# Keys of the first two tiles through unfolded weights, weights turned by DMA, layernorm roots in pairs, and a new port model in the scheduler, in a two-layer linear-attention and gated-MLP kernel

**Chip, cores, metric.** One core of one Trainium2 chip. The metric is the device time of one execution in microseconds (us), median of the runs; lower is better.

## The reference, cut to what matters

Inputs are bfloat16: x of 2048 x 512 (16 tiles of 128 rows), 32 heads of 16.

```python
def A(x, wqkv, w_phi, wo):                    # linear attention with learned features
    q, k, v = split(x @ wqkv)                 # heads of 16
    pk = k @ w_phi                            # per head 16 x 16; the same for q
    phi_k = concat(softmax(pk), softmax(-pk)) # 32 features a head
    kv = phi_k.T @ v ;  z = phi_k.sum(rows)   # sums over ALL 2048 rows
    return (phi_q @ kv) / (phi_q @ z + 1e-6) @ wo
def B(x, W_gate, W_up, W_down):
    return (relu(x @ W_gate) * (x @ W_up)) @ W_down
x += A(layernorm(x)); x += B(layernorm(x))
x += A(layernorm(x)); x += B(layernorm(x))
```

No query can be finished before the last of the sixteen key tiles is summed. The first key stage is therefore a wall: all attention outputs and the first gate matmul lie behind it.

## The kernel before

The kernel first records all its operations (engine, cost, priority, what they depend on, buffers). A list scheduler then sets the order on each engine with a cost model, and a table of some 2,100 priorities (DUE) found by search steers it. A string of bits (PLACE) says which of two engines takes each operation that can run on either. So a change of the model, the tables or one operation can move any instruction anywhere.

w_phi is folded into the key weights: `Wk2 = wk @ Wblk`, for which wk must be turned first. Before, TensorE turns it:

```python
k_fold = fold(wk, Wk2, l_wk, 100, 100, ("ACT", "DVE"))   # 16 turning matmuls, 4 copies ("hT<-b"),
                                                         # 16 folding matmuls, 4 copies ("Wk<-b")
def norm_A(l, t, due, after, how):            # one tile at a time
    a = stats(l, "A", t, due, after)          # VectorE: bn_stats, bn_aggr
    a = op("ACT", ACT1, due, lambda: nc.scalar.activation(out=ln[:, t:t + 1], in_=mv[:, t, 1:2], func=AF.Ln, ...
    a = op("ACT", ACT0, due, lambda: nc.scalar.activation(out=rs[:, t:t + 1], in_=ln[:, t:t + 1], func=AF.Exp, scale=-0.5)...
    n = op("DVE", SCALE, due, lambda: nc.vector.tensor_scalar(out=xn.t[:], in0=x_of(t), ...   # "xn"
    return turn(xn, ...)                      # tiles 0-3 by TensorE, the others by DMA from SyncE
class Keys:
    def tile(self, t, ...):
        k = op("PE", mm(4, 512), ...  kp = xnTA @ Wk2                    # "K"
        e = [op("ACT", act(512), ...  ek[s] = exp(+-kp)  for s in 0, 1   # "ek"
        v = op("PE", ... vp = xnTA @ wv ; evac(...)                      # "vext", ScalarE or VectorE
        a = op("DVE", SUM16, ...      sk = sum16(ek)                     # "sk", the softmax sums
        a = op("ACT", ...             sk = exp(-ln(sk))
        a = two multiplications phiK = ek * sk, each on VectorE or GpSimd
        z = op("PE", SUMS, ...        q += phiK.T @ vext                 # "kvz", the key sums
    def build(self, due):             # R: the key sums, laid out for the queries; 8 VectorE instructions
        for k in range(2):
            for s in range(2):
                made.append(op("DVE", ..., num, self.sums + [c_r1], ...)); made.append(op("DVE", DVE0, ..., den, ...))
def attend(...):                      # "erq" waits for all eight
    pe.append(op("PE", mm(len(groups), GE), due, ..., eq + made, [ps], name="erq"))
# the scheduler's port: one lock for VectorE's two-port forms and GpSimd
t = max(clock[e], o.ready, port if o.port else 0.0, ...);   port = t + occ
```

Cut: query projections, MLP, second layer, evacuations.

The softmax here doesn't subtract the row's maximum and nothing guards it: scores larger than these inputs give would overflow.

Of the kernel before, what the change touches and what calls it, by code (L numbers as in the profile page):

```python
# [8 lines left out]
P = 128  # L9
D = 512  # L10
H = 32
DH = 16
# [24 lines left out]
class Op:  # L37
# [3 lines left out]
    def __init__(self, eng, cost, due, emit, deps=(), takes=(), uses=(), name="", move=0, port=False,  # L41
                 follow=(), alt=None):
        self.eng, (self.occ, self.lat) = eng, cost
        self.due, self.emit, self.name, self.move, self.port = due, emit, name, move, port
        self.deps = [d for d in deps if d is not None]
        self.follow = [d for d in follow if d is not None]
        self.takes, self.uses = list(takes), list(uses)
        self.then, self.behind, self.alt, self.twin = [], [], alt, None
# [24 lines left out]
HOP = {"PE": 50, "ACT": 32, "DVE": 32, "POOL": 165, "SP": 90}  # L73
COLD = 3500
LANES = 8
# [3 lines left out]
def plan(ops):  # L79
# [14 lines left out]
    while len(order) < len(ops):  # L94
# [9 lines left out]
        for e, cand in open_.items():  # L104
            first, at = None, []
            for o in cand:
                t = max(clock[e], o.ready, port if o.port else 0.0, lanes[0] if o.move else 0.0)
# [11 lines left out]
            if first is None or (best is not None and first > best[0]):  # L119
                continue  # L120
            o = min((o for t, o in at if t <= first + 1), key=rank)
            came = max(clock[e], o.ready)
            if best is None or first < best[0] or came < best[1]:
                best = first, came, o
        assert best is not None, "no instruction can go"
        t, _, o = best
# [11 lines left out]
        if o.port:  # L138
            port = t + occ
# [68 lines left out]
SUMS = (8 * 40, 8 * 40 + 170)  # L208
# [4 lines left out]
XPOSE, XPOSE_LOADS = (1200, 3600), (1200, 3600)  # L213
# [3 lines left out]
def dma(nbytes):  # L217
    return 460, 2000 + nbytes / RATE


class K:
# [9 lines left out]
    "0000010100000000000000000000000001000000000001000000010000010000111000100010000011100010000000001100"  # L231
    "1110100001101000000001001111110001111111000111101111011101100100001001010011001101100101101011001010"
    "0111100111000000000111000001000000011010011000110100110100010010010010011111011011010111101111110001"
    "1"
)
PHI = dict(POOL=("POOL", "POOL"), DVE=("DVE", "DVE"), BOTH=("DVE", "POOL"))
PHI0 = ["POOL", "POOL", "DVE"] * 5 + ["BOTH"]
BLOCKS = ((1, 1, 2, 4, 4, 2, 2), (1, 1, 2, 4, 4, 2, 1, 1))
# [4 lines left out]
    171312045, 171176422, 171176382, 171108352, 171198950, 171077496, 171191852, 171044825, 171078679, 171078698,  # L243
    171075562, 172890511, 176979114, 171233483, 169157194, 169158347, 169158293, 172028606, 169159557, 172030067,
    175144900, 173911508, 175144538, 171845769, 169157815, 171893840, 172460034, 171325700, 171787868, 171042634,
    171000808, 171921057, 170984535, 171039910, 171020854, 171061543, 170544187, 171018809, 171804656, 171138113,
    171042055, 171921054, 166325450, 171843476, 171894266, 172913174, 172651099, 171841824, 172662070, 171803244,
    170856605, 171671995, 171013294, 171049523, 171011469, 170882211, 170861860, 170773832, 171088096, 171173941,
    166032751, 171021263, 171024027, 165980719, 171010636, 170972794, 170819202, 170901748, 170120315, 170882262,
    171029170, 171058781, 171028664, 170882214, 170773339, 170644736, 171176421, 170834144, 170500271, 171024600,  # L250
    171023816, 171671545, 170881567, 170973450, 170924320, 170862256, 171733328, 171027555, 171028689, 170104438,
    170987569, 171023551, 171017586, 170995073, 171010979, 171010010, 167097015, 171025767, 171021114, 170976230,
    171009963, 170940900, 170707416, 170903149, 170861679, 170895382, 170987736, 170805774, 171134539, 171029304,
    171015238, 170840189, 171086712, 170868324, 172856244, 171023850, 170972541, 170882265, 170862137, 170938874,
    171078382, 171074459, 171076295, 170781572, 171024964, 171027552, 170806858, 171027495, 171045955, 171031024,
    170994249, 171063885, 171044941, 170994211, 171021566, 171025728, 170861672, 170773342, 171004053, 171050973,
    171041308, 166032748, 171017859, 170995571, 172857251, 170995217, 171021462, 171036003, 171036000, 171021133,
    171034376, 171019328, 171026473, 170901529, 171024967, 170970509, 170994580, 171076245, 171039727, 174124623,
    167096153, 170995703, 170993965, 172856241, 171391510, 169375356, 166303781, 170203837, 171046298, 171045973,
    171020654, 171025772, 171029618, 171031289, 171018943, 171009668, 171040302, 212653769, 170870934, 170529933,  # L260
    171034876, 170993625, 171023605, 170674343, 170471544, 170946591, 173676712, 171046899, 170942347, 170973537,
    170992325, 171016031, 171004733, 170995129, 171046905, 171039117, 171046765, 170882142, 171036586, 171036549,
    170994607, 171035366, 171017772, 171035774, 166304101, 171351583, 171019187, 170346706, 170971352, 171020568,
    171004375, 171003406, 171019334, 170304741, 171357616, 166452149, 166304120, 171079347, 166362383, 171167760,
    171117024, 166253921, 166338723, 171040796, 171047078, 171026685, 169377831, 171021245, 170994356, 170993118,
    36276708, 36035224, 170174038, 170250060, 171018957, 171021288, 171052769, 171039826, 171052600, 171024073,
    170912232, 170912229, 171041278, 171041091, 171026709, 170998266, 170996907, 171023919, 171166970, 170791395,
    170174888, 36033968, 171014267, 166253845, 171052882, 170955784, 170370511, 171069861, 171052009, 171114979,
    171018524, 171021870, 166290380, 169376343, 170080981, 170529851, 171023791, 170744874, 36538735, 169932483,
    167242939, 166340952, 169222540, 171015285, 166253698, 171075807, 171049021, 171048078, 171040769, 171046830,  # L270
    170951770, 171034112, 171019616, 162145965, 166306292, 168062450, 170989765, 170738642, 171014079, 171052180,
    171053152, 171029348, 171107467, 171116988, 171052395, 171052101, 171047241, 171018507, 166291021, 170394652,
    170241606, 169841292, 169839339, 171025410, 36538707, 169011552, 170955744, 171035785, 170982203, 171011859,
    172910993, 171019677, 171107459, 171053563, 171019442, 170965939, 171116604, 170396198, 170371650, 170946958,
    170908940, 171025481, 169342071, 170739641, 170936868, 171053246, 171052141, 170955698, 171107296, 170969038,
# [183 lines left out]
def kernel(  # L459
# [14 lines left out]
    def pool(name, n, shape, dt=BF16, fifo=False):  # L474
        return Pool([new(f"{name}{i}", shape, dt) for i in range(n)], fifo)
# [541 lines left out]
```

## Time and profile before

| | before |
|---|---|
| median (range) of 3 runs | 387.88 us (387.75 to 388.2) |
| span of the profiled run | 386.3 us |
| first key sum step ("sk", VectorE) | 12.44 |
| first R instruction (VectorE) | 55.56 |
| first erq matmul (TensorE) | 57.98 |
| first gate matmul, "G1" (TensorE) | 68.28 |
| last matmul ends | about 383.1 |

Read it as a relay. The last three landmarks say when the key stage has let VectorE, then TensorE, then the MLP through. Behind G1 TensorE streams almost without a gap, so a microsecond gained at G1 should be one gained in the time. The views are in the prediction. First VectorE's early instructions in the kernel before, in order of time (start us, us, engine, line, operation, names, shapes, count, and in brackets the wait ahead):

```profile
6.20 1.29 DVE L605 CAST hT<-b 128x512 bf16<-128x512 f32 x2 [0.22 <-PE b L619]
7.41 1.28 DVE L651 BATCH_NORM_STATS2 bstA<-X 128x6 f32<-128x512 bf16 x2
...
12.44 1.21 DVE L693 TENSOR_REDUCE sk<-ek 128x64 f32<-128x1024 bf16 x1
```

SyncE's queue in the kernel before (start us, us, engine, line, operation, names, shapes, count, and in brackets the wait ahead):

```profile
5.10 5.21 SPq L614 DMA_TRANSPOSE hT<-in_A_wqkv_dram  x4
...
14.60 1.19 SPq L639 DMA_TRANSPOSE xnTA<-xn  x1
```

Four transposes (the query weights) are issued one after another, and the first x tile turned by DMA is issued at 14.60.

### The profile page before, as it was taken

The page shows a single profiled execution, that of the slowest core. Times are in us where ns is not written, and L with a number is a line of the kernel's source. Part 1 is how long each engine was busy: PE and PEld are TensorE (multiplying, and loading weights), DVE is VectorE, ACT ScalarE, POOL GpSimd, SP SyncE. Part 2 cuts the span into 40 slices and gives each one's busy share as a digit, 9 for nine tenths or more (in the row PEclk, how much of TensorE's full clock was granted, in tenths as well). Part 3 has the DMA queues.
Part 4 walks back from the last instruction along what each step waited for, and adds up shares of the span by engine and source line. Part 5 has one row for each costly group of instructions (what it writes and reads, how often), then busy time and mean ns, then how long its engine had stood idle before and what let it go on. Part 6 is the DMA issues. An engine that isn't in the chain of part 4 may idle for free.

```text
span 386.3 us, 7626 instructions
## 1 busy us (share of the span) xinstructions
PE 374.1 (97%) x2787; PEld 225.2 (58%) x2831; DVE 315.3 (82%) x799; ACT 212.0 (55%) x559; POOL 45.3 (12%) x46
## 2 busy tenths in 40 slices
PE   8989998999999999999999999999999999999996
PEld 4544454877654445445766755587865445447585
DVE  7999999999999889838875776899998999544244
ACT  5989988654456314554555669975435411422131
POOL 0433810000021000202222224000000000000000
PEclk9999999999999999999999999999999999999999
DMA  8469740232323224301101100013322234001020
GB/s 228 124 159 240 173 120 1 33 60 56 75 35 63 30 41 65 60 15 26 24 14 22 27 3 1 2 31 61 76 62 63 30 69 97 14 14 49 14 63 29
DMA packets 60869, 22.83 MB, mean 59 GB/s; under 512 B 52672, under 2 KB 59808, under 8 KB 60832
## 3 DMA queue, kind: packets, MB, share of 16 engines
q1 hardware_dynamic: 60416, 21.95, 26.2%
q8 instruction: 22, 0.36, 0.4%
q10 hardware_dynamic: 416, 0.39, 0.3%
q14 instruction: 15, 0.12, 0.1%
HBM read 7.91 MB, written 2.10 MB: 26 GB/s over the span
## 4 chain that ended last, share of the span: by engine, by line
PE 76%; DVE 9%; ACT 3%; issue 2%; DMA 2%; POOL 0%; DVEq 0%; ACTq 0%
PE b L874 34%; PE b L907 19%; PE b L810 6%; PE b L682 4%; PE b L688 4%; PE q L778 3%; PE b L850 2%; ACT Eq L764 2%; PE b L760 2%; DVE sk L693 2%; PE q L719 1%; DVE phiK L702 1%; DMA oT<-o 1%; DVE bstA L651 1%; DMA xnTA<-xn 1%
## 5 line engine op out<-in xcount | busy, mean ns | idle before, releaser
L874 PE MATMUL b<-xnTB,wgu 128*128 128x128 bf16 (+2 forms) x1192 | 150.1, 279 | 0.7 <-ACT xnTB L604 0.3
L874 PEld LDWEIGHTS <-wgu 128*128 128x128 bf16 x1200 | 97.3, 98 | 42.7 <-issue 0.4
L878 ACT ACTIVATE gu<-b 128x512 bf16<-128x512 f32 (+1 forms) x83 | 48.1, 584 | 67.0 <-PE b L874 63.0
L907 PE MATMUL b<-wd,hT 128*128 128x512 bf16 (+2 forms) x348 | 81.8, 372 | 0.8
L702 POOL TENSOR_TENSOR phiK<-ek,sk 128x512 bf16<-128x512 bf16 x40 | 44.6, 1133 | 191.3 <-ACT sk L698 106.1
L907 PEld LDWEIGHTS <-hT 128*128 128x128 bf16 (+1 forms) x363 | 34.5, 98 | 35.0 <-DVE hT L882 0.3
L882 DVE TENSOR_TENSOR hT<-gu 128x512 bf16<-128x512 bf16 (+1 forms) x83 | 33.5, 408 | 16.5 <-ACT gu L604 14.9
L685 ACT ACTIVATE ek<-b 128x512 bf16<-128x512 f32 x64 | 36.6, 626 | 14.1 <-PE b L682 14.0
L693 DVE TENSOR_REDUCE sk<-ek 128x64 f32<-128x1024 bf16 x32 | 38.6, 1208 | 6.8 <-ACT ek L685 5.8
L605 DVE CAST gu<-b 128x512 bf16<-128x512 f32 (+1 forms) x42 | 28.0, 669 | 15.7 <-PE b L874 15.7
L764 ACT ACTIVATE Eq<-b 128x512 bf16<-128x512 f32 x64 | 36.1, 631 | 1.7 <-PE b L760 0.9
L604 ACT CAST gu<-b 128x512 bf16<-128x512 f32 (+1 forms) x41 | 23.2, 565 | 22.8 <-PE b L874 21.8
L682 PE MATMUL b<-Wk,xnTA 128*128 128x512 bf16 x122 | 32.1, 379 | 1.6 <-DMA xnTA<-xn 1.2
L810 PE MATMUL b<-wo,oT 128*128 128x512 bf16 x125 | 32.4, 379 | 0.7 <-DMA oT<-o 0.4
L688 PE MATMUL b<-wv,xnTA 128*128 128x512 bf16 x120 | 31.9, 379 | 1.0 <-ACT xnTA L604 0.3
L760 PE MATMUL b<-xnTA,Wq 128*128 128x512 bf16 x125 | 30.9, 379 | 0.2
L914 DVE SCALAR_TENSOR_TENSOR X<-b,rsB,X 128x512 bf16<-128x512 f32 (+1 forms) x33 | 23.8, 730 | 7.5 <-PE b L907 7.2
L778 PE MATMUL q<-R,Eq 128*128 128x144 bf16 x256 | 27.8, 226 | 1.4 <-ACT DS L604 0.8
L604 ACT CAST N<-q 128x384 bf16<-128x384 f32 (+1 forms) x60 | 26.7, 466 | 4.1 <-DVE pr L803 2.9
L778 PEld LDWEIGHTS <-Eq 128*128 128x128 bf16 x256 | 20.3, 98 | 11.8 <-issue 2.2
L814 DVE TENSOR_TENSOR X<-X,b 128x512 bf16<-128x512 bf16 x32 | 21.4, 675 | 5.0 <-PE b L810 4.7
L855 ACT ACTIVATE gr<-b 128x192 bf16<-128x192 f32 (+1 forms) x19 | 5.8, 308 | 31.8 <-PE b L850 31.8
(70 smaller groups left out, 408.9 us busy)
## 6 DMA issues: line engine op xcount, KB each, us to landing
out_dram<-X SPq DMA_DIRECT2D x15, 128.0 KB, 1.8
X<-in_A_x_dram SPq DMA_DIRECT2D x6, 256.0 KB, 3.4
wgu<-in_B_W_gate_dram SPq DMA_DIRECT2D x4, 344.0 KB, 3.7
wgu<-in_B_W_up_dram SPq DMA_DIRECT2D x4, 344.0 KB, 3.6
wd<-in_B_W_down_dram SPq DMA_DIRECT2D x5, 256.0 KB, 4.9
wv<-in_A_wqkv_dram SPq DMA_DIRECT2D x2, 256.0 KB, 4.3
wo<-in_A_wo_dram SPq DMA_DIRECT2D x4, 128.0 KB, 3.4
oT<-o SPq DMA_TRANSPOSE x28, 2.4
```

Source lines behind the costliest of these rows:

```text
L604: both = {"ACT": ("ACT", act(cols), lambda: nc.scalar.copy(out=out_(), in_=in_()), False), "DVE": ("DVE", dve(cols), lambda: nc.vector.ten ...
L682: k = op("PE", mm(4, 512), due, lambda: [nc.tensor.matmul(kp.t[:], lhsT=xnTA[c][:, b, cols], rhs=Wk2[:, b, :], start=(b == 0), stop=(b == ...
L688: v = op("PE", mm(4, 512), due_v, lambda: [nc.tensor.matmul(vp.t[:], lhsT=xnTA[c][:, b, cols], rhs=wv[:, b, :], start=(b == 0), stop=(b == ...
L693: a = op("DVE", SUM16, due, lambda: nc.vector.tensor_reduce(out=sk.t[:], in_=ek.t[:].rearrange("p g s (h f) -> p (g s h) f", f=DH), axis=A ...
L702: e.tensor_tensor(out=ph.t[:].rearrange("p g s (h f) -> p (g s h) f", f=DH)[:, lo:lo + n], in0=ek.t[:].rearrange("p g s (h f) -> p (g s h) ...
L760: q = op("PE", mm(4, 512), due(c, b), lambda b=b, qp=qp: [nc.tensor.matmul(qp.t[:], lhsT=Wq2[:, m, b * P:(b + 1) * P], rhs=xnTA[c][:, m, : ...
L764: done.append(op("ACT", act(512), due(c, b), lambda b=b, s=s, qp=qp: nc.scalar.activation(out=Eq[c][:, b, s, :], in_=qp.t[:], func=AF.Exp, ...
L778: pe.append(op("PE", mm(len(groups), GE), due, lambda ps=ps, groups=groups: [nc.tensor.matmul(ps.t[:, n * GE:(n + 1) * GE], lhsT=Eq[c][:, ...
L810: a = op("PE", mm(4, 512), due + 3, lambda: [nc.tensor.matmul(yp.t[:], lhsT=oT.t[:, b, :], rhs=wo[:, b, :], start=(b == 0), stop=(b == NB ...
L874: nc.tensor.matmul(ps.t[:, q * W:(q + 1) * W], lhsT=wgu[:, s, b, g * P:(g + 1) * P], rhs=xT.t[:, b, 0:W], start=(b == 0), stop=(b == NB - 1))
L878: nc.scalar.activation(out=gu.t[:, 0, 0:cols], in_=gp.t[:, 0:cols], func=AF.Relu)
L907: nc.tensor.matmul(yp.t[:, 0:c1 - c0], lhsT=h.t[:m, f * W + i * P:f * W + (i + 1) * P], rhs=wd[:m, f, c0:c1], start=(f == 0), stop=(f == N ...
```

## The change

Intent: start the exponentials of the first keys without waiting for the fold, take the turning of wk off TensorE and its evacuations off ScalarE and VectorE, halve the number of small root instructions, and let the scheduler know better how VectorE and GpSimd share their port. Core of the diff (the priorities and the placement bits are all new, and cut; so are some further costs of the model, its rule for which engine is scheduled next, and refactorings without effect):

```diff
-HOP = {"PE": 50, "ACT": 32, "DVE": 32, "POOL": 165, "SP": 90}
+HOP = {"PE": 50, "ACT": 32, "DVE": 32, "POOL": 85, "SP": 90}
+ASKS, GIVES = (0, 0, 95, 15), (0, 20, 35, 135)
-                t = max(clock[e], o.ready, port if o.port else 0.0, lanes[0] if o.move else 0.0)
+                t = max(clock[e], o.ready, port - ASKS[o.port] if o.port else 0.0, lanes[0] if o.move else 0.0)
-            port = t + occ
+            port = t + occ - GIVES[o.port]
+UNFOLDED = 2
+PAIRN, PAIRK = 4, T            # roots of tiles 4.. in pairs; key roots stay single
-    k_fold = fold(wk, Wk2, l_wk, 100, 100, ("ACT", "DVE"))
+    k_fold = fold(A_wqkv[:, D:2 * D], Wk2, None, 10, 3000, ("ACT", "DVE"), True)     # turned by DMA, SyncE
+    def keys_unfolded(t, kp, xT, due):     # tiles 0, 1: KT = (x wk)^T, evacuate, K2 = KT^T Wblk
+        a = op("PE", mm(NB * NB, P), ..., name="KT")
+        a = evac("ACT", ..., "kT")
+        return op("PE", mm(NB, P), ..., name="K2")
-            out=ln[:, t:t + 1], in_=mv[:, t, 1:2], func=AF.Ln, scale=1.0, bias=eps[:]), ...
+            out=ln[:, t0:t0 + n], in_=mv[:, t0:t0 + n, 1], func=AF.Ln, scale=1.0, bias=eps[:]), ...
-            for k in range(2):
-                for s in range(2):         # the order in which R is built
+            for s in range(2):
+                for k in range(2):
-                ... for n, (b, s) in enumerate(groups)], eq + made, [ps], name="erq"))
+                ... for n, (b, s) in enumerate(groups)], eq + (made[4 * k:4 * k + 4] if k < 2 else made), [ps], name="erq"))
```

## The prediction

> **What bounds the kernel now.** I read the span and the busy shares first, then the busy time of each engine in windows, then TensorE's and VectorE's instructions in order of time around the end of the first key stage, and last the groups of VectorE in that stage.
>
> Page of the kernel before, first part:
>
> ```profile
> span 386.3 us, 7626 instructions
> PE 374.1 (97%) x2787; PEld 225.2 (58%) x2831; DVE 315.3 (82%) x799; ACT 212.0 (55%) x559; POOL 45.3 (12%) x46
> ```
>
> TensorE looks full everywhere, but matmul ends are modelled, so I count the work by columns instead. In the trace four 512-column matmuls start 0.86 us from the first to the next group's first (215 ns each), and 48 of 128 columns take 2.68 us in the chain of waits (56 ns each): columns/2.4 ns plus 2.5 ns. The built program of before has 2831 matmuls with 867,584 columns: 361.5 + 7.1 = 368.6 us. So of 386.3 us only 17.7 are not streaming. Where these lie, TensorE's instructions in order of time show:
>
> ```profile
> 55.36 2.75 PE L760 MATMUL b<-xnTA,Wq 128*128 128x512 bf16 x11
> 57.98 0.47 PE L778 MATMUL q<-R,Eq 128*128 128x144 bf16 x5
> ...
> 61.53 0.28 PE L778 MATMUL q<-R,Eq 128*128 128x144 bf16 x2 [0.78 <-ACT DS L604]
> ...
> 66.00 0.35 PE L778 MATMUL q<-R,Eq 128*128 128x144 bf16 x3 [0.36 <-DVE N L605]
> ...
> 68.28 2.84 PE L874 MATMUL b<-xnTB,wgu 128*128 128x128 bf16 x48 [0.30 <-ACT xnTB L604]
> ```
>
> The first query products (L778, "erq" below) start at 57.98 and the first gate matmul (L874, "G1") at 68.28. In the program's order 49.7 us of column work stand ahead of the first and 56.3 us ahead of the second, 312.2 us behind it. So 8.3 us are lost before erq, 3.6 between erq and G1 (57.98 to 68.28 is 10.3 for 6.7 of work). The last matmul ends at about 383.1, hence 383.1 - 68.3 - 312.2 = 2.6 us are lost in all the 315 us that follow, and 3.2 us are the tail. From G1 on TensorE is 99% full. The time is therefore **t(G1) + columns behind it + 2.6 + 3.2**, plus 1.6 from the span to the measured 387.88. A gain must come from an earlier G1, or from those 2.6.
>
> What holds G1? Busy time in windows (us; PE, PEld, DVE, ACT, POOL):
>
> ```profile
> 0.00:10.00 10.00, 8.43 (x51) 4.82 (x53) 7.15 (x26) 5.74 (x12) 0.70 (x6) 1.00 0.81 224
> 10.00:30.00 20.00, 18.64 (x132) 9.46 (x132) 19.92 (x39) 18.43 (x59) 8.38 (x8) 1.00 0.61 146
> 30.00:50.00 20.00, 19.75 (x144) 9.97 (x146) 19.65 (x32) 20.00 (x64) 11.89 (x11) 1.00 0.85 209
> 50.00:60.00 10.00, 9.14 (x73) 4.89 (x74) 9.01 (x21) 8.85 (x22) 0.48 (x1) 1.00 0.25 74
> 60.00:70.00 10.00, 7.91 (x85) 5.42 (x85) 9.66 (x34) 8.41 (x27) 0.00 (x0) 1.00 0.01 2
> ```
>
> VectorE is full from 10 to 50, ScalarE nearly so, GpSimd half idle. VectorE's end of the stage is this (order of time):
>
> ```profile
> 52.08 3.08 DVE L702 TENSOR_TENSOR phiK<-ek,sk 128x512 bf16<-128x512 bf16 x5
> 55.56 0.43 DVE L741 TENSOR_TENSOR R<-q,Mf 64x256 bf16<-64x256 f32 x1 [0.40 <-PE q L719]
> ```
>
> It finishes five feature multiplications, the last key sums run, then it builds R until 57.94 in eight instructions (55.56 to 57.94: 2.4 us), and erq starts 0.04 us later. From there a chain of small VectorE instructions (evacuation, m, reciprocal, w, pr, o) leads over two transposes to G1. VectorE's cost in the stage, groups up to 56 us and, last, the spread of one of them (min/median/max ns):
>
> ```profile
> L693 DVE TENSOR_REDUCE sk<-ek 128x64 f32<-128x1024 bf16 x16 | 19.1, 1201 | 0.3 <-ACT ek L685 0.3
> L702 DVE TENSOR_TENSOR phiK<-ek,sk 128x512 bf16<-128x512 bf16 x13 | 9.5, 769 | 0.0
> L662 DVE TENSOR_SCALAR xn<-X,mvA,rsA x16: 393/406/1121, 4.9 to 40.2; 128x512 bf16<-128x512 bf16 x16
> ```
>
> **What the Trainium skill says.** "Perfetto Trace Analysis", section Identifying the Most-Contended Engine, says that TensorE's busy share does not tell how near it is to its limit; the trace agrees (busy 97%, columns 95%, and the window 60 to 70 shows 7.91 busy for 6.0 us of columns). "TensorE: Matmul & The Clock Gate", section Back-to-back issue gap, gives N/2.4 + 2.5 ns for a warm array; the 215 and 56 ns above agree. "SBUF — State Buffer", section Who interferes with whom, says that VectorE and GpSimd share a port pair as an exclusive lock, and that two-port forms (tensor_scalar) and forms with two SBUF inputs against a reading GpSimd instruction block until the other ends, tensor_reduce never. The trace agrees: xn takes 0.41 us, but 1.09 and 1.12 us in the two cases that began as GpSimd had just started a multiplication (17.36 and 21.38); the reduction takes 1.20 us either way. That is 1.4 us lost on xn (16 x (492 - 406) ns), and the 13 multiplications average 769 ns where the five undisturbed ones take 3.08/5 = 616, some 2.0 us. This port is what the scheduler of the changed kernel models anew.
>
> **The change part by part.** Counts are from the two built programs; durations from the trace of before.
>
> Keys of tiles 0 and 1 through plain wk: per tile 16 x 128 columns replace 4 x 512 (the same), plus 4 x 128 and one ScalarE evacuation of 0.6 us. Folding by DMA: away go 16 transposing matmuls and four evacuations (two ScalarE 0.59, two VectorE 0.65), but four DMA transposes come on the queue of SyncE, at 1.3 us each there (5.10 to 10.31 for four). Filler matmuls go from 12 to 22. TensorE in sum: 871,680 columns and 2857 matmuls, 370.3 us, **1.8 more** than before, 2.2 of it filler, all ahead of G1. Behind G1 stand 312.6 us, +0.4.
>
> The intended head start is small. First exponential before at 10.77. After: xn at 5.3, transposed and out by 6.4, first step to 7.5, evacuated 8.1, second step, then vext and a root on ScalarE ahead of it in its order: about 9.5 (estimate). But VectorE has seven statistics, three xn and two copies in its order before its first reduction, some 7.2 us from 4.9, so that reduction starts near 12.1 instead of 12.44. And the folded wk is now ready later: eight DMA transposes in a row, the fourth landing near 12.8, the eighth near 18. TensorE can't run the first folded keys before about 15.5, when 11.8 us of its order are done. It is then 3.7 to 4.5 us behind its columns, as before (4.9 at the first key sum at 18.0). No gain there.
>
> VectorE up to the first R instruction: multiplications 13 to 9 (GpSimd 19 to 23): -4 x 0.62 = -2.5. Copies of the weight transposes -2 x 0.65, of the folded wk +2 x 0.65, of vext +2 x 0.6: +1.2. Sum **-1.3 us**. Fewer collisions: of 3.4 us lost I give it 1. ScalarE: six root pairs instead of twelve singles save 6 x (0.31 + 0.23) = 3.2, wk and vext evacuations -2 x 0.6 each, kT against the transposes' copies nothing: **-5.6 us**, so ScalarE is no more level with VectorE. R would start at 55.56 - 2.3 = 53.3.
>
> TensorE now joins as a bound: its order has 50.6 us ahead of the first erq, plus some 4.4 of start losses: not before 55.0.
>
> Order of R and finer waits: erq of the first half now waits for four of eight instructions, 1.2 us instead of 2.4. VectorE's order then has four evacuations (1.2) instead of six plus a 0.44 wait (1.75). From R to the first m: 3.6 instead of 4.57. The rest to G1 (two tiles of m to o at 2.2, residual, statistics, centring, transpose, evacuation) about 7.1: R to G1 10.7 against 12.72, **-2.0 us**.
>
> Taken together: erq limited by VectorE at 54.6, by TensorE at 55.0 or later; with a little of both 55.7. From erq to G1 9.5. G1 at 65.2 if the bounds add, 64.0 if only VectorE's counts; I take 64.7, **3.6 us earlier**. Behind it +0.4. The second layer's turn (240 to 250) has 1.2 us of gaps; the finer wait saves about 0.4 there. Time: 387.88 - 3.6 + 0.4 - 0.4 = **384.3**.
>
> **The rivals.** First, that the head start counts in full: ScalarE -5.6 and earlier keys would bring G1 to 61 and the time to about 381. For it: ScalarE is 20.00 of 20 busy from 30 to 50. Against it: VectorE was as full, gets only 1.3 us less, and TensorE's order can't reach G1 before 57.75 + 1.2 (start) + about 2 (cold array) = 61, so 378 is the least even with nothing lost later. Second, that SyncE's queue takes the place: the first x tile turned by DMA stands behind eight weight transposes and so is issued near 16 instead of 14.60. TensorE waited 1.17 us for such a tile at 26.14. If tiles 4 to 7 starve VectorE by 2 to 3 us, the gain is gone: 387. Against it: tiles 0 to 3 keep VectorE in work until about 18, and the tile lands by 19.5. Third, that the gain is given back in the pressed stretch 70 to 100, where VectorE is 29.92 of 30 busy: G1 earlier, but its followers wait. For it: so little slack. Against it: nine of 42 evacuations of gate and up move from VectorE to ScalarE (16.87 of 30 there), 6.0 us. It would leave 386.
>
> **Range and chances.** The two sides span 381 to 387.5, and every scheduling priority (the DUE table) is set anew, so losses after G1 may move by a microsecond either way: 381.5 to 387.2. Over 2% faster means under 380.1, hardly above the column bound of 378: 0.05. Over 2% slower needs 8 us lost in a schedule made for a better model: 0.01.
>
> **What would show it.** Right: the first R at 53 to 54.5, erq 1.2 to 1.6 us behind it, G1 at 64 to 65.5, after that at most 3 us of gaps, VectorE full from 12 to 53, ScalarE under 95% from 30 to 50. Wrong: idle VectorE between 14 and 24 waiting for xnTA by DMA (second rival); G1 at 61 to 62 (first); G1 early but gaps of over 4 us behind it (third); or xn and the multiplications blocked as often as before under 23 GpSimd ones.

## The result, and the profile after

After: median 387.29 us of 4 runs (386.79 to 387.49); before in the same rounds 388.04 (387.75 to 388.85). The ratio is 0.9975, 95% interval 0.9957 to 0.9994: the same within 2%, and 0.7 (by the medians) to 1.0 us (by the ratio) faster. Here and below a ratio is the mean time of one kernel's runs over that of the other's of the same rounds, so it is not quite the ratio of the medians quoted. Predicted was 384.3, range 381.5 to 387.2: the gain was a fifth to a quarter of the predicted 3.6 us, and the time lies just outside the range.

| us | before | after | predicted after |
|---|---|---|---|
| first key sum step (VectorE) | 12.44 | 13.65 | near 12.1 |
| first R | 55.56 | 55.27 | 53.3 |
| first erq | 57.98 | 56.97 | 55.7 |
| G1 | 68.28 | 66.84 | 64.7 |
| R to G1 | 12.72 | 11.57 | 10.7 |
| span | 386.3 | 385.5 | |

The page of the kernel after, first lines:

```profile
span 385.5 us, 7662 instructions
...
PE 374.3 (97%) x2811; PEld 225.8 (59%) x2857; DVE 312.8 (81%) x793; ACT 216.5 (56%) x555; POOL 39.4 (10%) x42
```

TensorE's instructions around the end of the key stage, after, in order of time:

```profile
55.11 1.89 PE L780 MATMUL b<-xnTA,Wq 128*128 128x512 bf16 x8
56.97 0.35 PE L798 MATMUL q<-R,Eq 128*128 128x144 bf16 x3
...
61.51 0.40 PE L641 MATMUL b<-ident,o 128*128 128x128 bf16 x4 [0.55 <-DVE o L826]
...
66.84 1.33 PE L894 MATMUL b<-xnTB,wgu 128*128 128x128 bf16 x21 [0.25 <-ACT xnTB L590]
```

erq starts 1.0 us earlier than before and G1 1.4. The program of after has 312.6 us of columns behind G1 (before 312.2), its last matmul ends at about 382.0, so 382.0 - 66.8 - 312.6 = 2.6 us are lost there, as before. From G1 on nothing was won or lost; what is missing is missing at G1. And most of it is missing at R already. VectorE at R, after:

```profile
51.75 3.08 DVE L722 TENSOR_TENSOR phiK<-ek,sk 128x512 bf16<-128x512 bf16 x5
55.27 0.42 DVE L761 TENSOR_TENSOR R<-q,Mf 64x256 bf16<-64x256 f32 x1 [0.44 <-PE q L739]
```

It is the same picture as before, 0.3 us earlier: five multiplications, a wait for the last key sums, R. Yet VectorE's work had shrunk as planned. Its groups up to 55.2 us, after (busy us, mean ns, then its idle time ahead and who ended most of it):

```profile
L650 DVE BATCH_NORM_STATS2 bstA<-X 128x6 f32<-128x512 bf16 x16 | 10.4, 680 | 3.2 <-DMA X<-in_A_x_dram 3.2
L665 DVE TENSOR_SCALAR xn<-X,mvA,rsA 128x512 bf16<-128x512 bf16 x16 | 6.7, 441 | 0.6 <-ACT rsA L660 0.6
L722 DVE TENSOR_TENSOR phiK<-ek,sk 128x512 bf16<-128x512 bf16 x9 | 6.6, 772 | 0.0
```

Before, xn cost 7.5 us at 492 ns and the 13 multiplications 9.5. Over all groups VectorE has 2.4 us less to do up to R (predicted 2.3). But 2.1 us of that came back as waits (all its waits together up to 56 us: 3.5 us before, 5.6 after). The waits of VectorE for x up to 56 us, first in the kernel before (us in total, times, longest):

```profile
DVE bstA L651 <- DMA X<-in_A_x_dram: 1.1, 1, 1.1
```

and in the kernel after:

```profile
DVE bstA L650 <- DMA X<-in_A_x_dram: 3.2, 3, 1.8
```

VectorE's early order of time after shows where (compare the same stretch of before above):

```profile
7.82 1.29 DVE L650 BATCH_NORM_STATS2 bstA<-X 128x6 f32<-128x512 bf16 x2 [1.79 <-DMA X<-in_A_x_dram]
...
13.65 1.19 DVE L703 TENSOR_REDUCE sk<-ek 128x64 f32<-128x1024 bf16 x1
```

The removed copies had run while VectorE would have waited for x anyway. And the fold's own copies now come at 12.98, just ahead of the first key sum step, which slips from 12.44 to 13.65. (Over the traces that keep before's early order, six of them, it lies at 11.9 to 12.4, and over nine with after's at 12.9 to 13.7; early landmarks vary by some 0.4 us from trace to trace.)

The other engines, as busy time in windows, after (us; PE, PEld, DVE, ACT, POOL, clock, DMA share, GB/s):

```profile
0.00:10.00 10.00, 8.10 (x47) 3.70 (x47) 5.46 (x22) 4.32 (x10) 0.70 (x6) 1.00 0.93 232
10.00:30.00 20.00, 19.11 (x147) 10.55 (x151) 19.76 (x39) 17.87 (x53) 9.15 (x9) 1.00 0.79 174
30.00:50.00 20.00, 19.47 (x150) 9.88 (x152) 19.43 (x31) 19.31 (x54) 15.28 (x15) 1.00 0.75 200
```

VectorE does 1.7 us less in the first 10 us, ScalarE falls from 20.00 to 19.31 in the third window. No engine is full, and all three are close to it. SyncE's queue after:

```profile
5.32 10.94 SPq L600 DMA_TRANSPOSE hT<-in_A_wqkv_dram  x8
16.37 1.19 SPq L638 DMA_TRANSPOSE xnTA<-xn  x1
```

Eight weight transposes occupy it until 16.26, and TensorE can fold only as the parts land. TensorE's start, after (L692 is the first key matmul on folded weights):

```profile
8.53 1.46 PE L584 MATMUL q<-zero 128*128 128x512 bf16 x6
10.56 0.88 PE L613 MATMUL b<-Wblk,hT 128*128 128x128 bf16 x8 [0.57 <-DMA hT<-in_A_wqkv_dram]
...
16.86 1.03 PE L692 MATMUL b<-Wk,xnTA 128*128 128x512 bf16 x4
```

Before, the first such matmul ran at 9.57. Counting columns of the matmuls that started in the first 15 us without the fillers on zeros, at the rate that the prediction gives, TensorE had done 7.7 us of useful work before (64 matmuls of 128 columns, 19 of 512) and 5.4 after (66 and 8). The head start itself is real: the first exponential runs at 9.42 instead of 10.77 (predicted 9.5). It is one tile's head start on an engine that then has to wait.

### The profile page after: what moved, and what is told of

It is laid out like the page before. It is cut to its first block, busy times and chain, and to the rows that moved or that the text cites. A ratio compares the mean times of both kernels' runs of the same rounds, so it can differ in the third digit from the quotient of the medians. Undisturbed runs are those within 1.5% of the kernel's fastest.

```text
span 385.5 us, 7662 instructions
## 1 busy us (share of the span) xinstructions
PE 374.3 (97%) x2811; PEld 225.8 (59%) x2857; DVE 312.8 (81%) x793; ACT 216.5 (56%) x555; POOL 39.4 (10%) x42
## 4 chain that ended last, share of the span: by engine, by line
PE 71%; DVE 17%; ACT 5%; DMA 3%; issue 3%; SPq 0%; DVEq 0%; ACTq 0%
PE b L894 31%; PE b L927 18%; PE b L830 5%; PE b L780 4%; PE b L698 4%; PE b L692 3%; PE q L798 3%; DVE sk L703 2%; PE b L870 2%; DVE bstA L650 2%; DMA xnTA<-xn 2%; PE q L739 1%; DVE xn L665 1%; DMA X<-in_A_x_dram 1%; DVE hT L902 1%
## 5 line engine op out<-in xcount | busy, mean ns | idle before, releaser
L894 PE MATMUL b<-xnTB,wgu 128*128 128x128 bf16 (+2 forms) x1192 | 152.0, 279 | 1.2 <-ACT xnTB L590 0.8
L927 PE MATMUL b<-wd,hT 128*128 128x512 bf16 (+2 forms) x347 | 84.4, 372 | 0.9
L722 POOL TENSOR_TENSOR phiK<-ek,sk 128x512 bf16<-128x512 bf16 x36 | 38.7, 1094 | 192.8 <-ACT sk L713 121.7
L902 DVE TENSOR_TENSOR hT<-gu 128x512 bf16<-128x512 bf16 (+1 forms) x83 | 34.6, 417 | 24.9 <-ACT gu L590 23.9
L590 ACT CAST gu<-b 128x512 bf16<-128x512 f32 (+1 forms) x51 | 29.1, 570 | 20.0 <-PE b L894 19.7
L590 ACT CAST N<-q 128x384 bf16<-128x384 f32 (+1 forms) x58 | 25.0, 452 | 12.2 <-PE q L798 10.6
L692 PE MATMUL b<-Wk,xnTA 128*128 128x512 bf16 x114 | 29.8, 379 | 0.7 <-DMA xnTA<-xn 0.4
L591 DVE CAST gu<-b 128x512 bf16<-128x512 f32 (+1 forms) x32 | 21.5, 676 | 7.7 <-PE b L894 7.5
L650 DVE BATCH_NORM_STATS2 bstA<-X 128x6 f32<-128x512 bf16 x32 | 21.4, 684 | 3.4 <-DMA X<-in_A_x_dram 3.2
```

The source lines that it names most:

```text
L590: both = {"ACT": ("ACT", act(cols), lambda: nc.scalar.copy(out=out_(), in_=in_()), False), "DVE": ("DVE", dve(cols), lambda: nc.vector.ten ...
L692: k = op("PE", mm(4, 512), due, lambda: [nc.tensor.matmul(kp.t[:], lhsT=xnTA[c][:, b, cols], rhs=Wk2[:, b, :], start=(b == 0), stop=(b == ...
L722: e.tensor_tensor(out=ph.t[:].rearrange("p g s (h f) -> p (g s h) f", f=DH)[:, lo:lo + n], in0=ek.t[:].rearrange("p g s (h f) -> p (g s h) ...
L894: nc.tensor.matmul(ps.t[:, q * W:(q + 1) * W], lhsT=wgu[:, s, b, g * P:(g + 1) * P], rhs=xT.t[:, b, 0:W], start=(b == 0), stop=(b == NB - 1))
L902: nc.vector.tensor_tensor(out=h.t[:, f0 * W:f0 * W + cols], in0=gu.t[:, 0, 0:cols], in1=gu.t[:, 1, 0:cols], op=Alu.mult)
L927: nc.tensor.matmul(yp.t[:, 0:c1 - c0], lhsT=h.t[:m, f * W + i * P:f * W + (i + 1) * P], rhs=wd[:m, f, c0:c1], start=(f == 0), stop=(f == N ...
```

## The experiments

In each experiment the order of instructions on every engine is the one that the kernel's own scheduler set, and only then is the edit made; otherwise the scheduler would answer the edit with another schedule. Names with a_ start from the kernel after, those with b_ from the kernel before. Each ran five or six times beside runs of the kernel before on the same chip. "R", "erq" and "G1" are the landmarks of its one profiled run; for reference 55.56, 57.98, 68.28 before and 55.27, 56.97, 66.84 after, with 0.9975 as after's ratio.

### First theory: VectorE lost its gain to late x loads

**a_x_early** issues the loads of x tiles 1 to 3 ahead of wv's:

```diff
+    early = [x_in[1], x_in[2], x_in[3]]
+    order = [o for o in order if o not in early]
+    n = order.index(l_wv[0])
+    order[n:n] = early
```

> The changed kernel, every engine's order kept, but the three single-tile loads X1 to X3 stand before the two loads of wv on SyncE's queue. Theory A (the saturated run of VectorE starts when the second x tile lands; the weight copies that the change removed from VectorE had filled that wait, so their 1.3 us were never to be had): the wait of 1.79 us at 7.82 falls to under 0.6, the first R instruction comes 0.8 to 1.5 us before 55.27, and the ratio to the kernel before falls from 0.9975 to about 0.995. Rival B (VectorE has slack later that is fed by TensorE and ScalarE, and the early wait is harmless): the wait falls, R stays within 0.3 us of 55.27, ratio 0.9975. Rival C: wv comes later and TensorE stalls in order, R later, ratio over 0.9985.

Measured: 387.55 us, ratio 0.9987 [0.9972, 1.0002]; R 55.57, erq 57.26, G1 67.14. The second statistics started at 5.82 instead of 7.82, and the waits for x fell from 3.2 to 2.4 us, yet R didn't come earlier. The chain that ended last, up to 58 us (start, us, what), passes through the DMA-turned weights and then TensorE:

```profile
11.98 4.47 DMA hT<-in_A_wqkv_dram
16.50 0.40 PE b L613 x4
17.34 0.86 PE b L692 x4
...
```

From 16.5 to about 41.6 that chain is TensorE's matmuls end to end. So removing VectorE's early wait doesn't bring R forward: something else holds it then.

**b_x_early** makes the same edit in the kernel before.

> The same move in the kernel before. Theory A: VectorE there copies weight transposes from 6.2 to 7.4 and waited nothing for X1, so the move gives little: first R within 0.4 us of 55.56, ratio 0.999 to 1.001. Rival B says the same; what would speak against A is a gain as large as in a_x_early.

Measured: 387.96 us, ratio 0.9997 [0.9985, 1.0009]; R 55.31, erq 57.73, G1 68.03. Nothing, within the scatter of traces.

**a_wk_act** takes two copies of folded wk (1.3 us) from VectorE to ScalarE:

```diff
+    for o in k_fold:
+        if o.eng == "DVE":
+            o.swap()
```

> The changed kernel, order kept, with the two copies of the folded wk that VectorE makes at 12.98 and 16.33 given to ScalarE: 1.3 us less on VectorE inside its saturated run. Theory A (work counts once the run has started): first R 0.8 to 1.3 us earlier, ratio about 0.995. Rival B (ScalarE, 19.31 of 20 busy from 30 to 50, or TensorE sets R): R within 0.3 us of 55.27 or later, ratio 0.9975 or higher.

Measured: 387.18 us, ratio 0.9975 [0.9962, 0.9989]; R 55.68, erq 57.37, G1 67.25. 1.3 us less on VectorE brought R no gain. The first theory falls: this work of VectorE does not set R. The trace shows where the 1.3 us went. TensorE:

```profile
16.20 0.40 PE L613 MATMUL b<-Wblk,hT 128*128 128x128 bf16 x4 [0.54 <-DMA hT<-in_A_wqkv_dram]
16.44 0.39 PE L641 MATMUL b<-ident,xn 128*128 128x128 bf16 x4
```

and VectorE:

```profile
16.93 0.69 DVE L591 CAST xnTA<-b 128x512 bf16<-128x512 f32 x1 [1.66 <-PE b L641]
```

TensorE folds a part of the query weights, turned by DMA (all four copies of folded wk had started by 15.91), and waits for it to land. Behind that, in its order, it turns the fourth x tile, and VectorE waits 1.66 us for that tile. The query weights' transposes stand behind the four of wk in SyncE's queue, where before they had it to themselves. The same pair of waits is in a_x_early (0.55 and 0.64 us) and in the traces of a_r_old, a_pe_plus, a_act_plus, a_roots_1 and the three a_..._minus runs below (0.4 to 1.2 and 0.5 to 1.5). In the kernel after itself VectorE copies that tile at 16.92 without a wait, since it is late by then for its own reasons. So work taken off VectorE ahead of some 17 us could gain nothing there. Whether R would follow if TensorE turned that tile ahead of the query fold was not run.

**a_r_old** builds R in the old order, so that erq waits for six of its eight instructions:

```diff
+    for l in range(2):
+        rs = [o for o in order if o.name in ("R", "Rz")][8 * l:8 * l + 8]
+        n = order.index(rs[0])
+        order = [o for o in order if o not in rs]
+        order[n:n] = [rs[i] for i in (0, 1, 4, 5, 2, 3, 6, 7)]
```

> The changed kernel with R built in the old order (both row halves of one buffer, then of the other) and all else kept. If the new order is worth what the prediction gave it (1.2 us from R to the first erq and on to the first gate matmul): first gate matmul 1 us later than 66.84, ratio about 1.000. If TensorE is busy with query matmuls until 56.97 anyway, so that the earlier release is not used: first gate matmul within 0.3 us of 66.84, ratio 0.997 to 0.998.

Measured: 387.57 us, ratio 0.999 [0.9978, 1.0002]; R 55.69, erq 57.48, G1 67.36. From R to G1 it takes 11.67 us against 11.57 after: the order of R is worth 0.1 us. In this run erq still waits for only six of the eight R instructions instead of four, so the wait for all eight was not tested. In the kernel after the eighth R instruction ends at 57.46, 0.5 us after erq started: that is about the most that the rest of the finer wait can give at erq. The 1.2 us that I had given it can't be had, and the lines of TensorE above show why: it has query matmuls to do from 55.11 to 56.97 whichever R instruction comes first, so the finer wait mostly frees a matmul that TensorE isn't ready for.

### Second theory: the engines are level; added work shows on any of them

**a_pe_plus** runs the four key matmuls of tiles 6 and 7 twice (1.73 us more TensorE):

```diff
-                    for b in range(NB)], [xT] + k_fold, [kp], name="K")
+                    for _ in range(2 if self.l == 0 and t in (6, 7) else 1) for b in range(NB)], [xT] + k_fold, ...
```

> Theory A (VectorE bounds the key stage) fell with the first four runs: X1 two us earlier, or 1.3 us less copying on VectorE, left the first R at 55.6 to 55.7. New theory P: once the folded keys can start, near 16.5, TensorE's column work sets the first erq; it is late by what TensorE can't do in the first 16 us. The changed kernel with the key matmuls of tiles 6 and 7 of the first layer issued twice (same result): 1.73 us more on TensorE. P: first erq 1.2 to 1.8 us after 56.97, time +1.2 to +1.8. Rival V (VectorE all the same, the early runs only showed orders that wait for each other): under 0.7. Rival S (TensorE, VectorE and ScalarE all level, none with slack): each of the three added costs shows about in full, 1.2 or more.

**a_dve_plus** runs one sk reduction (tile 6) and one statistics instruction (tile 9) twice (1.7 us more VectorE), **a_act_plus** the four exponentials of tiles 6 and 7 twice (1.96 us more ScalarE), with the same kind of edit:

```diff
+                for _ in range(2 if self.l == 0 and t == 6 else 1)]        # a_dve_plus, sk
+            for _ in range(2 if l == 0 and s == "A" and t == 9 else 1)]    # a_dve_plus, bn_stats
+                for _ in range(2 if self.l == 0 and t in (6, 7) else 1)]   # a_act_plus, ek
```

> The changed kernel with the key sum of tile 6 and the statistics of tile 9 computed twice: 1.71 us more on VectorE in the middle of its full stretch. P: first erq and time later by under 0.7 us. V: by 1.2 to 1.8. S: by 1.2 or more here and in the two sister runs.

> The changed kernel with both exponentials of tiles 6 and 7 computed twice: 1.96 us more on ScalarE. P and V: under 0.7 us later, as the pairing of roots gave ScalarE room. S: 1.3 or more.

| | us, median | ratio to before [95%] | R | erq | G1 |
|---|---|---|---|---|---|
| a_pe_plus | 388.7 | 1.0013 [0.9999, 1.0027] | 56.92 | 58.61 | 68.49 |
| a_dve_plus | 388.84 | 1.0029 [1.0003, 1.0056] | | | |
| a_act_plus | 389.33 | 1.0032 [1.0019, 1.0046] | 57.77 | 59.47 | 69.35 |

The profiled run of a_dve_plus was an outlier (391.4 us, granted clock 0.995; the other four 388.24 to 389.28), so its landmarks are not used; its ratio includes that run, and without it the ratio of the means would be 1.0014. TensorE's 1.73 us show as 1.65 at R, ScalarE's 1.96 as 2.5, and all three ratios lie 0.4 to 0.6% above 0.9975, that is 1.5 to 2.2 us. Added work costs about in full, wherever it is put. That fits "level". But a cost added to a link of a chain (exponential, sum, root, multiplication, key sum) also delays the chain, so adding alone can't tell an engine that is full from a chain that is tight.

**a_fold_pe** undoes the main part: wk is turned by TensorE again.

```diff
+    gone = [o for o in ops if o.name == "wT"][:4]        # the four DMA transposes of wk
+    order = [o for o in order if o not in gone]
+    # 16 matmuls with ident into the free q banks; two copies by VectorE, two by ScalarE
-                    idle(max(0, int((o.start - free - 150) / FILL)))
+                    idle(0)
```

> The changed kernel with wk for the fold turned by TensorE again (16 matmuls, two copies on VectorE in its wait for X1, two on ScalarE), the 14 fillers behind the first eight left out, all other orders kept: SyncE's queue has four weight transposes less, so that the waits of TensorE for weights turned by DMA (0.57 at 10.56, and the stream held until 16.5) go. P: first folded key matmul at 14.5 to 16 instead of 16.86, first erq 0.5 to 1.5 us earlier than 56.97, ratio 0.994 to 0.997. V or S: erq within 0.4 us of 56.97, ratio 0.997 to 0.999.

Measured: 387.92 us, ratio 0.9993 [0.998, 1.0005]; R 56.56, erq 58.25, G1 68.14: slower than after. The trace says why, and it isn't the fold. TensorE in order of time (L629 is the first step of the unfolded keys, 16 matmuls of 128 columns):

```profile
6.73 1.05 PE L629 MATMUL b<-xnTA,hT 128*128 128x128 bf16 x16
...
11.28 0.40 PE L644 MATMUL b<-ident,xn 128*128 128x128 bf16 x4 [1.50 <-DVE xn L668]
...
12.79 1.56 PE L629 MATMUL b<-xnTA,hT 128*128 128x128 bf16 x16
```

and its windows (PE first, the granted clock third from the end):

```profile
10.00:12.00 2.00, 0.40 (x4) 0.23 (x4) 2.00 (x5) 2.00 (x8) 0.00 (x0) 1.00 0.47 101
...
14.00:16.00 2.00, 2.00 (x12) 1.17 (x10) 2.00 (x5) 0.83 (x3) 0.00 (x0) 0.50 0.00 0
```

The same sixteen matmuls take 1.05 us at 6.73 and 1.56 at 12.79. With 0.40 us of matmuls from 10 to 12, the granted clock dropped to 0.50 (mean of the run 0.994). I had left out all filler matmuls but the first eight, and they kept the array warm. The run is confounded and says nothing of the fold.

### Taking work away

**a_dve_minus**, wrong (relative error 0.023), does the statistics of tiles 6 to 11 on half the row: 6 x (678 - 412) ns = 1.6 us less VectorE. **a_pe_minus**, still within the tolerance, leaves out one of four blocks in the keys of tiles 6 to 13: 1.7 us less TensorE. **a_all_minus**, wrong, does both and halves the exponentials of tiles 6 to 9 (1.7 us less ScalarE).

```diff
-            in_=x_of(t)
+            in_=x_of(t)[:, 0:256 if l == 0 and s == "A" and 6 <= t < 12 else D]          # VectorE
-                    for b in range(NB)], ...
+                    for few in [NB - 1 if self.l == 0 and 6 <= t < 14 else NB] for b in range(few)], ...  # TensorE
-                out=ek.t[:, :, s, :], ...
+                out=ek.t[:, 0:g, s, :], ...     # ScalarE: g=NG // 2 if self.l == 0 and 6 <= t < 10 else NG
```

> Wrong result on purpose (statistics over half the row for tiles 6 to 11 of the first layer). VectorE has 6 x 0.27 = 1.6 us less, ScalarE and TensorE the same; orders kept. Theory S (the three engines are level in the key stage and held together by in-order streams, so that a cost added to any one showed in full): taking from VectorE alone gives under half, ratio 0.995 to 0.9975. Theory V (VectorE is the bound): first R and time 1.2 to 1.6 us earlier, ratio about 0.9935.

> Wrong result on purpose (three of four blocks in the key matmuls of tiles 6 to 13): TensorE has 8 x 0.216 = 1.7 us less in the key stage. S: under half of it shows, ratio 0.995 to 0.9975. P (TensorE is the bound there): 1.2 to 1.7 us, ratio about 0.9935.

> Wrong result on purpose: both of the above, and the exponentials of tiles 6 to 9 over half the columns (8 x 0.21 = 1.7 us less on ScalarE). S: now most of 1.6 us shows, ratio 0.9925 to 0.994, and more than the two single runs together. If neither is so (one engine bounds), it equals the better of the two single runs.

| | us, median | ratio to before [95%] | R | erq | G1 |
|---|---|---|---|---|---|
| a_dve_minus | 387.44 | 0.9996 [0.9983, 1.0009] | 55.30 | 56.99 | 66.86 |
| a_pe_minus | 387.38 | 0.9985 [0.9972, 0.9999] | 55.65 | 57.34 | 67.22 |
| a_all_minus | 386.98 | 0.9976 [0.9964, 0.9989] | 54.32 | 56.01 | 65.88 |

The R line of a_dve_minus (VectorE, order of time) is the kernel after's to within 0.03 us:

```profile
55.30 0.41 DVE L762 TENSOR_TENSOR R<-q,Mf 64x256 bf16<-64x256 f32 x1 [0.59 <-PE q L740]
```

Measured at R, relieving VectorE alone or TensorE alone gives nothing, and relieving all three moves R and G1 by some 0.96 us. In a_dve_minus the chain from 15 to 56 us is some 72% TensorE lines. But the three traces also differ in when the stage gets going. The copy of the fourth turned x tile in a_all_minus (VectorE):

```profile
17.07 0.69 DVE L591 CAST xnTA<-b 128x512 bf16<-128x512 f32 x1 [0.77 <-PE b L641]
```

In a_dve_minus it runs at 17.61 and in a_pe_minus at 17.71, against 16.92 after: TensorE waits 1.13 and 1.20 us there for the turned query weights (0.41 in a_all_minus). From this copy to R it is 37.7 us in a_dve_minus, 37.9 in a_pe_minus and 37.3 in a_all_minus, against 38.35 after, and 38.1 to 38.3 in a_x_early, a_r_old and a_roots_1, which change no work of VectorE or TensorE. Counted so, VectorE alone gives some 0.7 us, TensorE alone 0.4 and all three 1.1. With one trace each, it is therefore not shown that only relieving all of them together helps; ScalarE alone and pairs of engines were not relieved.

The forecasts of the level theory missed in time. For a_all_minus it gave 0.9925 to 0.994; measured was 0.9976, no better than after's 0.9975, though R and G1 came earlier. The other two ratios lie above the ranges given as well. a_all_minus is 0.4 us below the other two by the medians; the intervals, some 1 us wide, don't decide whether that difference is real.

**a_fold_pe_xf** tries the fold by TensorE again, with the fillers kept, one spare bank, x loaded early and two statistics moved behind the second transposed tile:

```diff
+    early = [x_in[1], x_in[2], x_in[3]]                  # as in a_x_early
+    gone = [o for o in ops if o.name == "wT"][:4]
+    # turns and copies placed one by one; copies by VectorE, ScalarE, VectorE, VectorE
+    late = [order[at("stats", "DVE", k)] for k in (4, 5)]
```

> Mends a_fold_pe, whose missing fillers let the array fall back to half clock from 12.8 to 16.5 and whose stream waited 1.50 us for the second x tile: wk is turned by TensorE again, the fillers stay, X1 to X3 are loaded before wv, two statistics stand behind the second tile's normalization. If the late start of the folded keys (weights turned by DMA, eight in a row) is what cancels the gain of the change: first folded key matmul at 15.2 to 16.2 instead of 16.86, first R 0.5 to 1.3 us before 55.27, ratio 0.994 to 0.996. If the start isn't what binds: R within 0.3 us of 55.27, ratio 0.997 to 0.999.

Measured: 388.42 us, ratio 1.0017 [1.0005, 1.003]; R 57.37, erq 59.06, G1 68.94; the first key sum step only at 15.29. The array stayed warm, but my hand-made order stalls: VectorE waits 1.0 us for its weight copies and 0.8 for roots (0.6 of that is in every run), TensorE 1.1 for xn and 0.7 for kT. Inconclusive again about the fold.

### What bounded the kernel before?

By now I doubted the prediction's first reading too, and had an interim theory: that before, ScalarE (20.00 of 20 us busy from 30 to 50) and not VectorE was the bound.

**b_pe_plus**, **b_dve_plus**, **b_act_plus** make the same additions in the kernel before (edits as above).

> The kernel before with the key matmuls of tiles 6 and 7 of the first layer issued twice: 1.73 us more on TensorE. The prediction held that VectorE alone bounds the key stage of this kernel: then under 0.6 us shows, ratio 0.999 to 1.0015. If its engines were already level: 1.2 us or more, ratio 1.003 to 1.005.

> The kernel before with the key sum of tile 6 and the statistics of tile 9 computed twice: 1.71 us more on VectorE. Both theories: 1.2 to 1.8 us, ratio 1.003 to 1.005.

> The kernel before with both exponentials of tiles 6 and 7 computed twice: 1.96 us more on ScalarE. VectorE alone the bound: under 0.8, ratio up to 1.002. Level: 1.3 to 2.2, ratio 1.0035 to 1.006.

**a_roots_1** emits the roots of the paired tiles singly again, at the same places:

```diff
-            out=ln[:, t0:t0 + n], in_=mv[:, t0:t0 + n, 1], ...
+            out=ln[:, u:u + 1], in_=mv[:, u:u + 1, 1], ...) for u in range(t0, t0 + n)]      # rs likewise
```

> The changed kernel with the six paired layernorm roots issued as twelve single ones again, order kept: some 3.2 us more on ScalarE between 13 and 40. Level engines, ScalarE among them: 2 to 3.2 us later than the changed kernel, ratio 1.003 to 1.006, so that the pairing would be what pays for the rest of the change. If ScalarE has room from the change (the prediction's reading): under 1 us, ratio below 1.000.

**b_act_minus** and **b_dve_minus** take 1.7 us from ScalarE (exponentials of tiles 6 to 9 halved) and 1.6 us from VectorE (half-row statistics, tiles 6 to 11; wrong, error 0.023) of the kernel before, with the edits shown for the kernel after. The result of b_act_minus stayed within the tolerance.

> Wrong result on purpose: the kernel before with the exponentials of tiles 6 to 9 of the first layer over half the columns, 8 x 0.21 = 1.7 us less on ScalarE. The three b_ runs suggest that ScalarE, not VectorE, holds its key stage, and that VectorE and TensorE have about 1 us of slack there: then first R 0.6 to 1.3 us before 55.56 and ratio 0.9965 to 0.9985. If VectorE holds it after all: R within 0.3 us, ratio 0.9993 to 1.0007.

> Wrong result on purpose: the kernel before with statistics over half the row for tiles 6 to 11, 1.6 us less on VectorE. ScalarE the bound: first R within 0.3 us of 55.56, ratio 0.9993 to 1.0007. VectorE the bound, as the prediction had it: R 1 to 1.6 us earlier, ratio 0.996 or lower.

| | us, median | ratio to before [95%] | R | erq | G1 |
|---|---|---|---|---|---|
| b_pe_plus | 388.54 | 1.0007 [0.9994, 1.0019] | 56.30 | 58.72 | 69.02 |
| b_dve_plus | 388.91 | 1.0015 [1.0001, 1.0029] | 56.15 | 58.58 | 68.87 |
| b_act_plus | 390.32 | 1.0051 [1.0038, 1.0063] | 57.98 | 60.40 | 70.70 |
| b_act_minus | 387.92 | 0.9989 [0.9967, 1.001] | 55.37 | 57.79 | 68.09 |
| b_dve_minus | 386.74 | 0.9958 [0.9941, 0.9975] | 53.94 | 56.37 | 66.67 |
| a_roots_1 | 387.15 | 0.9972 [0.9958, 0.9987] | 55.43 | 57.12 | 66.99 |

The additions to the kernel before pointed to ScalarE: 1.96 us more there moved R by 2.4, while TensorE's and VectorE's moved it by 0.7 and 0.6. The removals say the opposite. The R line of b_act_minus:

```profile
55.37 0.43 DVE L741 TENSOR_TENSOR R<-q,Mf 64x256 bf16<-64x256 f32 x1 [0.40 <-PE q L719]
```

and of b_dve_minus:

```profile
53.94 0.43 DVE L742 TENSOR_TENSOR R<-q,Mf 64x256 bf16<-64x256 f32 x1 [0.40 <-PE q L720]
```

1.7 us less on ScalarE: nothing beyond the scatter. 1.6 us less on VectorE: R and G1 1.6 earlier and the time 0.42% (1.6 us) shorter. The waits say the same: from its first key sum step to R VectorE waits 0.72 us in all in the kernel before, and the same 0.72 in b_act_minus. The kernel before was bound by VectorE, as the prediction had read it. My interim theory falls. That the 1.6 us show in full is partly luck: in b_dve_minus the xn instructions also took 415 ns on average instead of 492 (1.2 us in all), and VectorE waited 1.1 us more between its first key sum step and R.

In b_act_plus VectorE waits 1.26 us at 30.74 and 1.08 at 36.42, and the trace puts both down to layernorm roots of ScalarE; neither wait is in the trace of before. The doubled exponentials thus delayed what VectorE needs next, though ScalarE wasn't the bound: the addition tested the chain, not the engine. That VectorE's own addition moved R by only a third has two reasons in its trace. Its first key sum step happened to run at 11.86 instead of 12.44, and xn took 447 ns instead of 492 (0.7 us in all). From the first key sum step to R it takes 44.29 us against 43.12, with the same 0.72 us of waits.

a_roots_1 has after's ratio to within 0.0003: pairing the roots is worth nothing that these runs can show.

## Why the prediction was wrong, point by point

**The reading of the kernel before: right.** VectorE set R, and behind G1 TensorE streams; VectorE waits only 0.72 us from its first key sum step to R, and in b_dve_minus R, G1 and the time all move by the same 1.6 us.

**The failing step: "R would start at 55.56 - 2.3 = 53.3".** The work term was right (2.4 us less, with fewer multiplications and cheaper xn). The step from work to time failed: R moved by 0.3, because VectorE waits 2.1 us more. Two things came in its place. First, the prediction let VectorE work without a pause, "some 7.2 us from 4.9, so that reduction starts near 12.1". But the next tile of x came only at 7.82, after a wait of 1.79 us, and the reduction started at 13.65. The copies of turned wk (1.3 us) had filled that wait in the kernel before, so taking them out made it longer (1.1 to 3.2 us in total for x). Second, even with less to wait for x, R stayed: loading x earlier (a_x_early) or taking 1.3 us of copies off VectorE (a_wk_act) left R at 55.6 to 55.7; in both traces VectorE then waits at about 17 us for TensorE, which stands at the query weights turned by DMA. The 2.3 us had been priced as if nothing but its own work held VectorE on the way to R.

**TensorE's bound, the term "some 4.4 of start losses": too small.** At the first key sum matmul after (19.03) TensorE was 5.05 us behind its columns, and at the first erq 56.97 - 50.6 = 6.4. I had seen that the folded keys couldn't start before about 15.5 (they started at 16.86) and still concluded "no gain there" where it should have been "a loss". And I took the larger of two bounds plus 0.7. What sets R from 17 us on in the kernel after is only in part known: VectorE waits just 1.2 us of the 38.35 from there to R, yet taking 1.6 us off it (a_dve_minus) shows there as 0.7, and TensorE and ScalarE are nearly full too. A sum per engine is a lower bound and was used as an estimate.

**R to G1, "-2.0": it was -1.15.** From R to erq it fell by 0.72 (2.42 to 1.70 us) where 1.2 was claimed for the finer wait; I had priced the wait of erq without asking what TensorE would do in that time. The order of R gave 0.1 of it (a_r_old). The rest is likely the finer wait and the new order of evacuations and centring behind it: R to the first m fell from 4.57 to 3.83 us (predicted 3.6), and from there to G1 from 8.15 to 7.74 (predicted 7.1). Which of them gave how much was not isolated.

**ScalarE "-5.6 us": the 3.2 for paired roots was an error of method.** I multiplied mean durations, but instructions that follow each other overlap: with the roots single again (a_roots_1) ScalarE's root instructions are busy 7.3 us up to R, against 5.3 after, so 2.0 and not 3.2. ScalarE's window from 30 to 50 shrank by 0.7 (to 97%, where I had said under 95%), and in a_roots_1 undoing the pairing cost no time that shows.

**Behind G1: "+0.4" right, "-0.4" in the second layer's turn did not come**: the loss there is 2.6 us in both kernels. The tail went from 3.2 to 3.5, so that 1.4 earlier at G1, less 0.4 columns and 0.3 of tail, leaves about the 0.8 us by which the span fell.

**The rivals.** The first (head start in full) is wrong, though the head start itself came as predicted. The second (SyncE's queue) is partly right: the eight weight transposes in a row delayed the fold and the first DMA-turned x tile, to 16.37. VectorE did not stand idle between 14 and 24 in the kernel after (0.24 us of waits); but once it came earlier, as in a_wk_act, it waited at 17 us, for the weights on that queue rather than for x tiles. The third (given back later) is wrong: VectorE is 28.41 of 30 busy from 70 to 100 after, 29.92 before, and no new gaps followed.

**What stays open.** How much the late fold, of wk and of the query weights, costs by itself: both kernels with the fold of wk back on TensorE brought stalls of their own, and the query fold was not moved. What the new port model is worth by itself: xn became cheaper (441 ns instead of 492), the multiplications on VectorE did not (772 instead of 769), and no run separates it from the new order. No experiment beats both kernels with a right result; a_roots_1 and a_wk_act equal the kernel after. b_dve_minus suggests that relieving VectorE in the kernel before, without delaying the fold, would be worth about as much as is taken away; that was not built.

## What to carry to other kernels

Before pricing work taken from the bounding engine, ask what that work was standing in: copies that fill a wait for a load are worth nothing, and once the engine is relieved by a microsecond or two the next thing in another engine's order may hold it. To find the bound, take work away rather than add it, because an added cost in a chain shows whether or not its engine is full; then look in the trace at where the engine waits, because the gain can come back as a wait elsewhere. A finer wait is worth only what the waiting engine would do with it.

## What the Trainium skill lacked or had wrong

- "Perfetto Trace Analysis", section Identifying the Most-Contended Engine, names the engine with the highest occupancy as the one to work on first. Over the key stage of the kernel before, 10 to 50 us, that is VectorE (39.57 of 40 us busy; ScalarE 38.43), and the runs agree: 1.6 us less on VectorE gave 1.6, and 1.7 less on ScalarE nothing. From 30 to 50 alone it would have been ScalarE (20.00 of 20; VectorE 19.65), which led me to the interim theory. The page has no test by taking work away, which told the two apart.
- "TensorE: Matmul & The Clock Gate", section What's actually happening, puts the fall to the cold clock after at least one idle window of about 3.4 us; its section A second HAM failure mode tells of frequent short idles without a size. In a_fold_pe no single wait was longer than 1.50 us: two bursts of 0.40 us between 9.8 and 12.4 were all that TensorE ran, and the granted clock was 0.80 from 12 to 14 and 0.50 from 14 to 16. So in this trace a sparsely used stretch of 2.6 us was followed by the half clock, with no idle window as long as the page's; the shortest stretch that does it was not measured. In a_fold_pe_xf, with the filler matmuls on zeros kept, the mean granted clock was 1.0.
